# Gate weights folded into the second product of a fused attention and two-MoE kernel

## The chip, the cores and the metric

One core of a Trainium2 chip runs the whole program. The metric is the device time of one execution in microseconds. The kernel before took 864.77, 860.23 and 864.11 us in three runs, median 864.11.

## The reference

Three layers follow each other on 3072 tokens of 384 numbers, in float32:

```python
f = 1 / (1 + exp(-f_logit))                     # (4, 8, 768, 48)
state = f[t][..., None] * state + outer(k[t], v[t])
y[t] = q[t] @ state                             # -> x, (3072, 384)

h = x @ w_in                                    # (384, 2048)
g = h * sigmoid(h)
x2 = g @ w_out                                  # (2048, 384)

logits = x2 @ w_gate                            # (384, 8)
e = argmax(logits);  p = softmax(logits)[e]
out = p * (relu(x2 @ w1[e]) @ w2[e])            # (8, 384, 1024), (8, 1024, 384)
```

The logits are a linear function of g: logits = g @ (w_out @ w_gate). An argmax decides which expert a token gets, so they are computed to about float32's precision.

## The kernel before

**Tiles and groups.** The 24 chunks of 128 tokens are worked on in nine groups, of 2, 2, then six times 3, then 2 chunks (0 to 8). The 2048 columns of w_in, and the rows of w_out, are cut into 16 pieces of 128. Every weight of the MoE layers, and every operand that meets one, is split into a rounded part hi and a rest lo, and each product is three matmuls: hi with lo, lo with hi, hi with hi.

**Slots.** The main loop runs over 144 slots (g, i), a group and a piece: the first 8 pieces of group 0, all 16 of group 1, the other 8 of group 0, then groups 2 to 8. A slot s does `moe_h` (nine matmuls ph for the piece of w_in; 256 or 384 token columns), then the steps that the table `plan` has for s, then `moe_g` (SiLU on ACT and VectorE, and its split gh, gl), then `moe_o` of slot s − 2 (for each tile of the group three matmuls px of 384 columns with the pieces of w_out), then the steps of the table `after`. `plan` is filled by `at(s, ...)` and `after` by `at_end(s, ...)`: attention stages of a later group, loads and splits of weight pieces (`load_piece`; f is the attention's gate input, in_raw and out_raw the raw weight pieces), and the logits. TensorE's instructions keep this written order. The other engines' order is set by the tile framework's scheduler; each engine's queue runs in order, SyncE's loads too.

**Logits.** When a group's last piece is done, `moe_x2` (called at the end of `moe_o`) copies each px times 0.5 into x2 (the SiLU's factor 2 is undone there). For groups 0 to 7 the tiles are then turned one a slot by `flip_rows` (three transposes plt, one ACT copy rt) and at the slot's end multiplied with the gate weights wgc by `gate` (three float32 matmuls of 8 columns, which the chip runs as six passes, and a VectorE copy into lgt). `pick` (argmax, softmax) comes after the last tile's slot, `route` four slots later (rank within the expert, then scatter of the rows by GpSimd into the token buffer xs). Group 8's two tiles get their logits in the tail by `logits_pe` and `logits_pe2`.

**Token buffer.** xs in DRAM has 4096 rows of 388 numbers. Eight transfers of 512 rows (`prefill`) fill it with an empty row, zrow, issued on SyncE's queue from slots 21, 23, ... 35 on of the plan.

**Tail.** A string, TAIL, orders what follows slot 143. Its letters: T start and turn the rows of the first expert's first part ("head", pxs_h), o one `moe_o`, f one up-product (nine matmuls p_h) or down-product (24 matmuls po_h) of the head, l and m the logits of group 8, p `pick`, r `route`, w the load of a second expert's first matrix, k the rank, g the fetch of the rest's rows (xe_r), t their turn (pxs_r), F what is left of f. In `route`, pr is the counting product on TensorE. Then `moe2` runs all the other experts (p_r is the rest's first product).

**Weight tiles.** `new_unit` takes hi and lo of four pieces from one ring of 16 tiles, "wt". zrow, the turned rows rt and the head's buffers hh share the tile "big" at different times.

Of the kernel before, what the change touches and what calls it, by code (L numbers as in the profile page):

```python
# [9 lines left out]
F32 = mybir.dt.float32  # L10
# [14 lines left out]
EARLY = 6  # L25
TB = 'xah'
HB = 'xah'
LB = 'x'
RT = 3
RD = 4  # L30
FA = 1
# [9 lines left out]
KACT = 7  # L41
ND = 1
MO = 'oeh'
TAIL = 'TooflfmfpfrffwgfkfftF'
KW = -14
HF0 = 137
FX = 0
# [19 lines left out]
WE = -6  # L67
WS = -1
PF = 20
PFD = 2  # L70
GACT = 9
PR = 1, 0, 1, 0, 1, 0, 1, 0
PRD = 2
# [18 lines left out]
def kernel(  # L92
# [50 lines left out]
    ends = dram.tile([NCH, DM], F32, name="ends")  # L143
    xs = dram.tile([E * CAP, ROW], F32, name="xs")

    ident = const.tile([P, P], F32, name="ident")
# [14 lines left out]
    big = late.tile([P, 6 * 512], F32R, tag="big", name="big")  # L161
    xt0 = [big[:, i * 2 * DM : (i + 1) * 2 * DM].rearrange("p (r c t) -> p r c t", r=2, c=KC) for i in range(2)]
    zrow = big[:, 4 * DM : 4 * DM + ROW].bitcast(F32)
    BANKS = {0: "haahhaaa", 1: "haahhaaa"}

    def use(n, i, name):
# [31 lines left out]

    def new_unit(key):
        kind = key[0]  # L200
        full = [P, 4, KC, P] if kind in ("in", "w1") else [P, 4, DM]
        nm = "_".join(str(x) for x in key)
        units[key] = tuple(wts.tile(full, F32R, tag="wt", name=f"{nm}_{x}") for x in ("hi", "lo"))

    def part_of(src, kind, i, n):
        cols = slice(i * P, (i + n) * P)
# [2 lines left out]
    def load_raw(t, src, kind, i, eng):  # L209
# [12 lines left out]
    def split(key, h, x, lo_engine):  # L222
        hi, lo = units[key]
        (keep(nc.scalar.copy) if key == ("w1", 1, 1) and RT > 1 else nc.scalar.copy)(hi[:, h], x)  # L224
        lo_engine.tensor_sub(lo[:, h], x, hi[:, h].bitcast(F32))  # L225
# [280 lines left out]
    def moe_o(g, i):  # L506
        hi, lo = gt.pop((g, i))
        first, last = ((0, HF), (HF - 1, NF - 1)) if g == 0 else ((0,), (NF - 1,))
        wh, wl = units["out", i // 4]
        if i in first:  # L510
            px[g] = [bank("x", f"px_{g}_{t}") for t in range(sizes[g])]
        for t in range(sizes[g]):
            o = px[g][t][:, :DM]
            m = slice(t * P, (t + 1) * P)
            pe.matmul(o, hi[:, m], wl[:, i % 4, :], start=i in first, stop=False)
            pe.matmul(o, lo[:, m], wh[:, i % 4, :], start=False, stop=False)
            pe.matmul(o, hi[:, m], wh[:, i % 4, :], start=False, stop=i in last)
# [6 lines left out]
    def moe_x2(g, i):  # L524
        lgt[g] = att.tile([P, sizes[g], E], F32, tag="lg", name=f"lg_{g}", bufs=2)
        for t in range(sizes[g]):
            n = starts[g] + t
            if n in x2:
                nc.vector.scalar_tensor_tensor(
                    out=x2[n][:, :DM], in0=px[g][t][:, :DM], scalar=0.5, in1=x2[n][:, :DM], op0=ALU.mult, op1=ALU.add  # L530
                )
                r = x2[n]
            else:
                r = att.tile([P, ROW], F32, tag="x2", name=f"x2_{n}", bufs=5)
                x2[n] = r
# [8 lines left out]
    rts = []  # L544

    def logits_pe(g):
        for t in range(sizes[g]):
            r = x2[starts[g] + t]
            pt = bank("a", f"plt_{g}_{t}")
            for c in range(KC):  # L550
                pe.transpose(pt[:, c * P : (c + 1) * P], r[:, c * P : (c + 1) * P], ident)
            rt = att.tile([P, KC, P], F32, tag="sg", name=f"rt_{g}_{t}", bufs=SG)
            (keep(nc.scalar.copy) if t % 2 < RT - 1 else nc.vector.tensor_copy)(rt.rearrange("p c t -> p (c t)"), pt[:, :DM])
            rts.append(rt)

    def logits_pe2(g):
        for t, rt in enumerate(rts):
            pl = bank(LB, f"plg_{g}_{t}")
            for c in range(KC):
                pe.matmul(pl[:, :E], rt[:, c, :], wgc[:, c, :], start=c == 0, stop=c == KC - 1)  # L560
            nc.vector.tensor_copy(lgt[g][:, t, :], pl[:, :E])
# [4 lines left out]
    def flip_rows(g, t):  # L566
# [2 lines left out]
        for c in range(KC):  # L569
            pe.transpose(pt[:, c * P : (c + 1) * P], r[:, c * P : (c + 1) * P], ident)  # L570
        if not turned_rows:
            turned_rows.append(late.tile([P, 4, KC, P], F32, tag="big", name="rt"))
        rt = turned_rows[0][:, (starts[g] + t) % 4]
        nc.scalar.copy(rt.rearrange("p c t -> p (c t)"), pt[:, :DM])
        flipped[g, t] = pt, rt

# [221 lines left out]
    def head_start():  # L798
        w = HEAD * P
        xt_hl = [att.tile([P, CPG, KC, P], F32R, tag=f"xt{x}", name=f"xe{x}_h", bufs=2) for x in "hl"]  # L800
        flat = [x.rearrange("p r c t -> p (r c t)") for x in xt_hl]
        big = late.tile([P, 8 * DM], F32R, tag="big", name="hh_h")
        more = [att.tile([P, DM], F32R, tag=x, name=f"{x}_h") for x in ("ep", "en")]
        slots = [big[:, i * w : (i + 1) * w] for i in range(8 * DM // w)]
# [7 lines left out]
    def rest_fetch():  # L812
# [5 lines left out]
        x = wts.tile([P, 2, KC, w], F32R, tag="wt", name="x_r")  # L818
        items["rest"] = dict(nm="r", e=0, w=w, rows=lambda t: r[t], x=[x[:, i] for i in range(2)])

    def moe2(m2):
# [310 lines left out]
    assert s0 + RD < len(seq)  # L1132
    at(HF0, head_fetch)
# [32 lines left out]
    nc.scalar.preload_act_table_set("natural_log_exp_and_others")  # L1166
    consts()
    total = NG * NF
    for s in range(first, total):
        if s >= 0:  # L1170
            moe_h(*seq[s])
# [30 lines left out]
    for c in TAIL:
# [48 lines left out]
```

## Time and profile before

| | before |
|---|---|
| median of three runs | 864.11 us (860.23 to 864.77) |
| profiled execution, its own time | 862.22 us |
| span of the profiled execution | 860.5 us |
| mean granted clock of TensorE | 0.976 |
| TensorE busy | 824.1 us, 96%, 5684 matmuls |
| VectorE busy | 490.9 us, 57% |
| ACT busy | 383.8 us, 45% |
| GpSimd busy | 107.7 us, 13% |
| DMA | 95.93 MB, mean 111 GB/s |

The span is the profiled part of one execution; what lies around it is 1.7 us. Busy time of a matmul counts from its start to its modelled end, and neighbours overlap, so the price of one in a full stream is the step between two starts. [...] PE in a row is TensorE, DVE VectorE, ACT ScalarE, POOL GpSimd, SP or SPq SyncE's queue. L328 is the one line that issues all of TensorE's products, L333 the one for transposes, so rows are told apart by their tiles.

### The profile page before, as it was taken

The page shows a single profiled execution, that of the slowest core. Times are in us where ns is not written, and L with a number is a line of the kernel's source. Part 1 is how long each engine was busy: PE and PEld are TensorE (multiplying, and loading weights), DVE is VectorE, ACT ScalarE, POOL GpSimd, SP SyncE. Part 2 cuts the span into 40 slices and gives each one's busy share as a digit, 9 for nine tenths or more (in the row PEclk, how much of TensorE's full clock was granted, in tenths as well). Part 3 has the DMA queues.
Part 4 walks back from the last instruction along what each step waited for, and adds up shares of the span by engine and source line. Part 5 has one row for each costly group of instructions (what it writes and reads, how often), then busy time and mean ns, then how long its engine had stood idle before and what let it go on. Part 6 is the DMA issues. An engine that isn't in the chain of part 4 may idle for free.

```text
span 860.5 us, 15378 instructions
## 1 busy us (share of the span) xinstructions
PE 824.1 (96%) x5684; PEld 786.9 (91%) x5684; DVE 490.9 (57%) x1290; ACT 383.8 (45%) x803; POOL 107.7 (13%) x136
## 2 busy tenths in 40 slices
PE   6789899999999999999999999999999999999994
PEld 3689899989999999999999999998998999999994
DVE  5898786546566665666567547354456336336520
ACT  5554654353353444435345333355355335335520
POOL 2001000001102001001001101045301110110011
PEclk9779989999999999999999999999999999999998
DMA  9755990222343343344333312214182425525400
GB/s 202 166 147 140 295 240 16 45 42 72 88 103 102 77 99 103 75 93 110 75 82 98 94 52 75 91 38 157 47 274 86 160 77 186 164 81 191 164 26 27
DMA packets 166436, 95.93 MB, mean 111 GB/s; under 512 B 115692, under 2 KB 159965, under 8 KB 166352
## 3 DMA queue, kind: packets, MB, share of 16 engines
q1 hardware_dynamic: 162224, 83.80, 37.3%
q0 software_dynamic: 3280, 9.49, 3.0%
q10 hardware_dynamic: 848, 1.57, 0.6%
q8 instruction: 46, 0.75, 0.4%
q14 instruction: 38, 0.31, 0.1%
HBM read 75.61 MB, written 16.33 MB: 107 GB/s over the span
## 4 chain that ended last, share of the span: by engine, by line
PE 70%; DMA 10%; DVE 6%; issue 5%; ACT 4%; SPq 2%; POOL 1%; POOLq 0%; DVEq 0%; ACTq 0%
PE px L328 20%; PE ph L328 19%; PE po L328 8%; PE p L328 7%; PE py L328 4%; DMA out_dram<-o,oi 3%; DMA f<-in_f_logit_dram 2%; PE sc L328 2%; DMA in_raw<-in_moe_w_in_dram 2%; DMA w_raw<-in_moe_w_dram 2%; PE plt L328 1%; PE pl L328 1%; PE p_r L328 1%; PE po_r L328 1%; PE pxs L333 1%
## 5 line engine op out<-in xcount | busy, mean ns | idle before, releaser
L492 ACT ACTIVATE se<-ph 128x384 f32<-128x384 f32 (+1 forms) x144 | 65.3, 454 | 166.7 <-PE ph L328 162.6
L328 PE MATMUL px<-out_lo,gh 128*128 128x384 f32 x384 | 137.4, 358 | 1.5 <-ACT gh L502 1.2
L494 DVE SCALAR_TENSOR_TENSOR sg<-se,ph 128x384 f32<-128x384 f32 (+1 forms) x144 | 73.0, 507 | 105.6 <-ACT se L492 104.9
L328 PE MATMUL px<-out_hi,gl 128*128 128x384 f32 x384 | 130.8, 341 | 0.6 <-DVE gl L503 0.5
L328 PE MATMUL px<-out_hi,gh 128*128 128x384 f32 x384 | 130.4, 340 | 0.0
L328 PE MATMUL ph<-xtl,in_hi 128*128 128x384 f32 (+1 forms) x384 | 126.0, 328 | 0.0
L328 PE MATMUL ph<-xth,in_lo 128*128 128x384 f32 (+1 forms) x384 | 124.5, 324 | 0.8 <-DVE in_lo L225 0.8
L328 PE MATMUL ph<-xth,in_hi 128*128 128x384 f32 (+1 forms) x384 | 124.7, 325 | 0.0
L503 DVE TENSOR_TENSOR gl<-sg,gh 128x384 fp32r<-128x384 f32 (+1 forms) x144 | 79.9, 555 | 34.1 <-ACT gh L502 33.1
L502 ACT CAST gh<-sg 128x384 fp32r<-128x384 f32 (+1 forms) x144 | 68.6, 477 | 67.4 <-DVE sg L494 64.0
L328 PEld LDWEIGHTS px<-out_lo,gh 128*128 128x128 f32 x384 | 73.0, 190 | 4.4 <-ACT gh L502 1.9
L328 PEld LDWEIGHTS px<-out_hi,gl 128*128 128x128 f32 x384 | 73.3, 191 | 1.1 <-DVE gl L503 1.1
L328 PEld LDWEIGHTS ph<-xth,in_lo 128*128 128x128 f32 x384 | 72.9, 190 | 1.2 <-DVE in_lo L225 1.1
L328 PEld LDWEIGHTS px<-out_hi,gh 128*128 128x128 f32 x384 | 72.9, 190 | 0.0
L328 PEld LDWEIGHTS ph<-xtl,in_hi 128*128 128x128 f32 x384 | 72.8, 190 | 0.0
L328 PEld LDWEIGHTS ph<-xth,in_hi 128*128 128x128 f32 x384 | 72.8, 190 | 0.0
L328 PE MATMUL po<-w_lo,hh 128*128 128x384 f32 (+6 forms) x200 | 67.8, 339 | 0.0
L328 PE MATMUL po<-w_hi,hh 128*128 128x384 f32 (+6 forms) x200 | 67.3, 336 | 0.0
L328 PE MATMUL po<-w_hi,hl 128*128 128x384 f32 (+6 forms) x200 | 67.3, 336 | 0.0
L224 ACT CAST w_hi<-w_raw 128x384 fp32r<-128x384 f32 x124 | 57.1, 513 | 21.7 <-DMA w_raw<-in_moe_w_dram 19.0
L225 DVE TENSOR_TENSOR w_lo<-w_raw,w_hi 128x384 fp32r<-128x384 f32 x104 | 52.7, 552 | 10.8 <-ACT w_hi L224 10.5
L328 PE MATMUL p<-xsl,w_hi 128*128 128x480 f32 (+6 forms) x168 | 58.5, 348 | 0.0
(239 smaller groups left out, 1537.7 us busy)
## 6 DMA issues: line engine op xcount, KB each, us to landing
w_raw<-in_moe_w_dram SPq DMA_DIRECT2D x64, 384.0 KB
xs<-big SPq DMA_DIRECT2D x8, 776.0 KB
out_again<-in_moe_w_out_dram SPq DMA_DIRECT2D x16, 384.0 KB
xe<-xs SPq DMA_DIRECT2D x7, 776.0 KB
out_raw<-in_moe_w_out_dram SPq DMA_DIRECT2D x13, 384.0 KB
f<-in_f_logit_dram SPq DMA_DIRECT2D x24, 192.0 KB
k<-in_k_dram SPq DMA_DIRECT2D x24, 192.0 KB
q<-in_q_dram SPq DMA_DIRECT2D x24, 192.0 KB
```

The costliest lines, as they stand in the source:

```text
L224: (keep(nc.scalar.copy) if key == ("w1", 1, 1) and RT > 1 else nc.scalar.copy)(hi[:, h], x)
L225: lo_engine.tensor_sub(lo[:, h], x, hi[:, h].bitcast(F32))
L328: ins = nc.tensor.matmul(*a, **k)
L333: ins = nc.tensor.transpose(*a, **k)
L492: nc.scalar.activation(e, ph[:, :GT], AF.Tanh, scale=0.5)
L494: nc.vector.scalar_tensor_tensor(out=t, in0=e, scalar=1.0, in1=ph[:, :GT], op0=ALU.add, op1=ALU.mult)
L502: (nc.scalar.copy if g < GACT else nc.vector.tensor_copy)(hi, t)
L503: (nc.gpsimd if (g, i) < LOV else nc.vector).tensor_sub(lo, t, hi.bitcast(F32))
```

## The change

- Each tile of w_out (`new_unit`, kind "out") gets eight more columns, filled with w_out @ w_gate. For each of the 16 pieces `fold_turn` multiplies hi and lo as stationary operand with an identity (six matmuls of 128 columns, so the piece is turned and its halves are added), ACT copies the result into one of two tiles wturn, and `fold_gate` multiplies it with wgc (three float32 matmuls of 8 columns, six passes), after which ACT writes the hi and VectorE the lo of the eight columns. Turns are planned for slots 3 to 10 and 19 to 26, gates for the same slots' ends.
- From group 2 on `moe_o` moves 392 columns, and `moe_x2` takes the logits out of the last eight with one VectorE instruction a tile. `flip_rows` and `gate` stay for groups 0 and 1; `logits_pe` and `logits_pe2` are gone. `pick` and `route` of groups 2 to 7 come three slots earlier.
- `prefill` begins with a GpSimd subtraction that writes a spare column of zrow and reads the last pieces of w_in or w_out; the fills' slots are one apart instead of two.
- The ring of 16 weight tiles becomes two of 8 ("wa" for w_in and w1, "wb" for w_out and w2), "big" is cut into "big" and "side", the identity is made in wturn and copied, and wgc is loaded before slot 0.
- The head's start and turn move from the tail into slot 143, and TAIL is reordered: the letters l and m go, both down-products of the head come after the turn of the rest.

```diff
-TAIL = 'TooflfmfpfrffwgfkfftF'
+TAIL = 'ofofpffrffwgffktfF'
-PFD = 2
+PFD = 1
+PW = (0, 0, 1, 1, 2, 2, 3, 3)
-    wts = main.enter_context(tc.tile_pool(name="wts", bufs=16))
+    wts = main.enter_context(tc.tile_pool(name="wts", bufs=8))
...
+    zrow = side[:, :ROW]
+    spare = side[:, DM + 2 : DM + 3]
+    wturn = [side[:, ROW + i * DM : ROW + (i + 1) * DM] for i in range(2)]
...
-        full = [P, 4, KC, P] if kind in ("in", "w1") else [P, 4, DM]
+        full = [P, 4, KC, P] if kind in ("in", "w1") else [P, 4, DM + E if kind == "out" else DM]
+        tag = "wa" if kind in ("in", "w1") else "wb"
...
+    def fold_turn(i):
+        u, h = divmod(i, 4)
+        pt = bank("a", f"pe_{i}")
+        for c in range(KC):
+            for j, part in enumerate(units["out", u]):
+                pe.matmul(
+                    pt[:, c * P : (c + 1) * P], part[:, h, c * P : (c + 1) * P], identr, start=j == 0, stop=j == 1
+                )
+        nc.scalar.copy(wturn[i % 2], pt[:, :DM])
+        folding[i] = pt
+
+    def fold_gate(i):
+        u, h = divmod(i, 4)
+        hi, lo = (a[:, h, DM : DM + E] for a in units["out", u])
+        o = folding.pop(i)[:, DM : DM + E]
+        for c in range(KC):
+            pe.matmul(o, wturn[i % 2][:, c * P : (c + 1) * P], wgc[:, c, :], start=c == 0, stop=c == KC - 1)
+        nc.scalar.copy(hi, o)
+        nc.vector.tensor_sub(lo, o, hi.bitcast(F32))
...
-            o = px[g][t][:, :DM]
+            w = DM if g < 2 else DM + E
+            o = px[g][t][:, :w]
-            pe.matmul(o, hi[:, m], wl[:, i % 4, :], start=i in first, stop=False)
+            pe.matmul(o, hi[:, m], wl[:, i % 4, :w], start=i in first, stop=False)
...
+            if g >= 2:
+                nc.vector.tensor_scalar(
+                    out=lgt[g][:, t, :], in0=px[g][t][:, DM : DM + E], scalar1=0.5, scalar2=None, op0=ALU.mult
+                )
...
-        for t in range(sizes[g]):
-            at(s0 + t, flip_rows, g, t)
-            at_end(s0 + t, gate, g, t)
-        s0 += sizes[g]
+        if g < 2:
+            for t in range(sizes[g]):
+                at(s0 + t, flip_rows, g, t)
+                at_end(s0 + t, gate, g, t)
+            s0 += sizes[g]
...
+    for i in range(NF):
+        at(i + (3 if i < HF else 11), fold_turn, i)
+        at_end(i + (3 if i < HF else 11), fold_gate, i)
...
-    at(6, lambda: nc.sync.dma_start(out=wgc, in_=moe2_w_gate.rearrange("(c p) e -> p c e", p=P)))
+    at(-4, lambda: nc.sync.dma_start(out=wgc, in_=moe2_w_gate.rearrange("(c p) e -> p c e", p=P)))
...
     def prefill(i):
+        lo = units["in", 3][1][:, :, 0, :1] if i % 2 == 0 else units["out", 3][1][:, :, :1]
+        tc.keep_in_program_order(
+            nc.gpsimd.tensor_sub(spare, lo[:, PW[i]].bitcast(F32), lo[:, PW[i]].bitcast(F32))
+        )
...
+    at(total - 1, head_turn)
```

The order of instructions at three places, before and changed.

TensorE at the end of slot 4, in group 0 or 1, before: the last ph, the six px of slot 2, the first ph of slot 5.

```order
L328 MATMUL ph_4_762<-big,in_hi 128x256
L328 MATMUL px_0_703<-out_lo,gh_2_699 128x384 [waits Activation_49]
L328 MATMUL px_0_703<-out_hi,gl_2_700 128x384 [waits DVE_49]
L328 MATMUL px_0_703<-out_hi,gh_2_699 128x384
L328 MATMUL px_1_704<-out_lo,gh_2_699 128x384
L328 MATMUL px_1_704<-out_hi,gl_2_700 128x384
L328 MATMUL px_1_704<-out_hi,gh_2_699 128x384
L328 MATMUL ph_5_786<-big,in_hi 128x256 [waits DVE_49]
```

Changed: the last two of the fold's six turn matmuls (pe), the same px, the gate passes of the fold, the first ph of slot 5.

```order
L355 MATMUL pe_792<-identr,out_hi 128x128
L355 MATMUL pe_792<-identr,out_lo 128x128
L355 MATMUL px_0_706<-out_lo,gh_2_702 128x384
L355 MATMUL px_0_706<-out_hi,gl_2_703 128x384 [waits DVE_49]
L355 MATMUL px_0_706<-out_hi,gh_2_702 128x384
L355 MATMUL px_1_707<-out_lo,gh_2_702 128x384
L355 MATMUL px_1_707<-out_hi,gl_2_703 128x384
L355 MATMUL px_1_707<-out_hi,gh_2_702 128x384
L355 MATMUL pe_792<-wgc,side 128x8 [waits Activation_49]
L355 MATMUL pe_792<-wgc,side 128x8 x2
L355 MATMUL ph_5_815<-big,in_hi 128x256 [waits DVE_49]
```

Between ph and px stand six matmuls more, and behind px the gate passes, with a wait for ACT; ph of slot 5 is behind them.

TensorE in the tail, before: the end of the first down-product po_h, the turn of the rest's rows pxs_r, the start of the second po_h.

```order
L328 MATMUL po_h_7486<-w_0_1_lo,hh_h 128x384 [waits Activation_49,Pool_49]
L328 MATMUL po_h_7486<-w_0_1_hi,en_h 128x384 [waits DVE_49]
L328 MATMUL po_h_7486<-w_0_1_hi,hh_h 128x384
L333 MATMUL pxs_r_7518<-ident,xe_r_7440 128x128 [waits DMAHW4_49]
L333 MATMUL pxs_r_7518<-ident,xe_r_7441 128x128 [waits DMAHW5_49]
L333 MATMUL pxs_r_7523<-ident,xe_r_7440 128x128 [waits PE_49]
L333 MATMUL pxs_r_7523<-ident,xe_r_7441 128x128
L333 MATMUL pxs_r_7528<-ident,xe_r_7440 128x128
L333 MATMUL pxs_r_7528<-ident,xe_r_7441 128x128
L328 MATMUL po_h_7533<-w_0_0_lo,hh_h 128x384
```

Changed: the end of the last up-product p_h, pxs_r, the first po_h.

```order
L355 MATMUL p_h_7513<-xel_h,w_0_1_hi 128x256
L355 MATMUL p_h_7513<-xeh_h,w_0_1_lo 128x256
L355 MATMUL p_h_7513<-xeh_h,w_0_1_hi 128x256
L360 MATMUL pxs_r_7542<-identr,xe_r_7496 128x128 [waits DMAHW4_49]
L360 MATMUL pxs_r_7542<-identr,xe_r_7497 128x128 [waits DMAHW5_49]
L360 MATMUL pxs_r_7547<-identr,xe_r_7496 128x128 [waits DVE_49,PE_49]
L360 MATMUL pxs_r_7547<-identr,xe_r_7497 128x128
L360 MATMUL pxs_r_7552<-identr,xe_r_7496 128x128 [waits DVE_49]
L360 MATMUL pxs_r_7552<-identr,xe_r_7497 128x128
L355 MATMUL po_h_7557<-w_0_0_lo,hh_big 128x384 [waits Activation_49]
L355 MATMUL po_h_7557<-w_0_0_hi,hh_side 128x384
```

A down-product that stood ahead of the turn, which waits for the fetch's transfers, now stands behind it.

SyncE's queue at the fills, before: f, q and k of attention, five of the fills (xs<-big), and weight pieces of w_in between and behind them.

```order
L191 DMA q_1089<-in_q_dram 128x8x48 [waits DMAHW4_49,DVE_49]
L191 DMA f_1665<-in_f_logit_dram 128x8x48 [waits DMAHW5_49]
L1143 DMA xs<-big 128x4x388 [waits DMAHW6_49]
L1143 DMA xs<-big 128x4x388 [waits DMAHW7_49]
L1143 DMA xs<-big 128x4x388 [waits DMAHW0_49]
L219 DMA in_raw<-in_moe_w_in_dram 96x3x256 [waits DMAHW1_49,DVE_49]
L220 DMA in_raw<-in_moe_w_in_dram 32x3x256 [waits DMAHW2_49]
L1143 DMA xs<-big 128x4x388 [waits DMAHW3_49]
L1143 DMA xs<-big 128x4x388 [waits DMAHW4_49]
L219 DMA in_raw<-in_moe_w_in_dram 96x3x256 [waits DMAHW5_49,DVE_49]
L220 DMA in_raw<-in_moe_w_in_dram 32x3x256 [waits DMAHW6_49]
L351 DMA a_all<-ends 48x4x1 [waits DMAHW7_49]
```

Changed: the last loads around slots 20 to 30, seven of the fills (xs<-side), and one v load among them.

```order
L195 DMA q_1859<-in_q_dram 128x8x48 [waits DMAHW4_49,DVE_49]
L378 DMA a_all<-ends 48x4x1 [waits DMAHW5_49,DMAHW2_49]
L378 DMA a_all<-ends 48x4x1 [waits DMAHW6_49]
L222 DMA out_raw<-in_moe_w_out_dram 128x768 [waits DMAHW7_49,DVE_49]
L1169 DMA xs<-side 128x4x388 [waits DMAHW0_49,Pool_49]
L1169 DMA xs<-side 128x4x388 [waits DMAHW1_49,Pool_49]
L1169 DMA xs<-side 128x4x388 [waits Pool_49]
L1169 DMA xs<-side 128x4x388 [waits DMAHW3_49,Pool_49]
L195 DMA v_1907<-in_v_dram 128x8x48 [waits DMAHW4_49,PE_49]
L1169 DMA xs<-side 128x4x388 [waits DMAHW5_49,Pool_49]
L1169 DMA xs<-side 128x4x388 [waits DMAHW6_49,Pool_49]
L1169 DMA xs<-side 128x4x388 [waits DMAHW7_49,Pool_49]
```

Each fill waits for GpSimd, whose queue has these rows: the empty row is made, then one subtraction for each fill, from the second on behind the DMA of the fill before.

```order
L1161 MEMSET side 128x388 [waits Pool_49]
L1162 MEMSET side 128x1 [waits Pool_49]
L1167 TENSOR_TENSOR side<-in_lo 128x1 [waits DVE_49]
L1167 TENSOR_TENSOR side<-out_lo 128x1 [waits DMAHW7_49,DVE_49,Pool_49]
L1167 TENSOR_TENSOR side<-in_lo 128x1 [waits DMAHW0_49,Pool_49]
L1167 TENSOR_TENSOR side<-out_lo 128x1 [waits DMAHW1_49,DVE_49,Pool_49]
```

The fills have moved behind the last weight piece (out_raw) but for the first, and v and k loads stand behind or between them.

## Rows read from the trace of the kernel before

**Rows 1.** The page's slices, 40 of 21.5 us: TensorE's busy tenths, granted clock, DMA share

```profile
PE   6789899999999999999999999999999999999994
...
PEclk9779989999999999999999999999999999999998
DMA  9755990222343343344333312214182425525400
```

**Rows 2.** Stretches: length; busy PE, PEld, DVE, ACT, POOL; granted clock; DMA share, GB/s

```profile
80.00:100.00 20.00, 20.00 (x166) 19.76 (x167) 18.47 (x50) 11.42 (x28) 1.73 (x4) 1.00 0.90 239
100.00:120.00 20.00, 17.50 (x111) 16.98 (x108) 13.06 (x30) 11.44 (x21) 0.00 (x0) 0.83 1.08 310
```

**Rows 3.** Groups of instructions, ACT: busy us, mean ns, idle before and releaser

```profile
L574 ACT COPY rt<-plt 128x384 f32<-128x384 f32 x22 | 10.5, 476 | 3.5 <-PE plt L333 3.5
```

**Rows 4.** TensorE's timeline in a slot of group 3: start us, us, instruction

```profile
240.10 0.34 PE L328 MATMUL px<-out_lo,gh 128*128 128x384 f32 x1
...
240.62 0.73 PE L328 MATMUL plt<-wgc,rt 128*128 128x8 f32 x6
241.20 0.42 PE L328 MATMUL ph<-xtl,in_hi 128*128 128x384 f32 x1
241.46 0.34 PE L328 MATMUL ph<-xth,in_lo 128*128 128x384 f32 x1
...
242.85 0.49 PE L333 MATMUL plt<-ident,x 128*128 128x128 f32 x3
243.10 0.42 PE L328 MATMUL px<-out_lo,gh 128*128 128x384 f32 x1
243.35 0.33 PE L328 MATMUL px<-out_hi,gl 128*128 128x384 f32 x1
```

**Rows 5.** The same view in a slot of group 8, whose chunks are two

```profile
555.87 0.28 PE L328 MATMUL ph<-xtl,in_hi 128*128 128x256 f32 x1
...
556.22 0.28 PE L328 MATMUL ph<-xtl,in_hi 128*128 128x256 f32 x1
```

**Rows 6.** TensorE's waits: total us, times, longest

```profile
PE plt L328 <- ACT rt L574: 2.9, 2, 1.9
...
PE px L328 <- ACT gh L502: 1.2, 2, 1.0
PE ph L328 <- DVE in_lo L225: 0.8, 1, 0.8
PE pk L333 <- ACT qt L375: 0.7, 1, 0.7
PE px L328 <- DVE gl L503: 0.5, 1, 0.5
PE pxs_r L333 <- DMA xe_r<-xs: 0.5, 1, 0.5
```

**Rows 7.** TensorE's timeline, products of qt with the state

```profile
326.17 1.03 PE L328 MATMUL py<-qt,state 112*112 112x128 f32 x8
327.13 0.31 PE L328 MATMUL py<-am,v 128*48 128x128 f32 x1
```

**Rows 8.** SyncE's timeline at three of the fills: start us, us

```profile
98.30 2.53 SPq L1143 DMA_DIRECT2D xs<-big  x3
```

**Rows 9.** The chain there, a weight piece: start us, us, what

```profile
102.28 6.97 DMA in_raw<-in_moe_w_in_dram
```

**Rows 10.** Stretches of the hole, columns as in group 2

```profile
100.00:104.00 4.00, 1.50 (x16) 1.09 (x12) 3.58 (x7) 2.58 (x3) 0.00 (x0) 1.00 1.04 368
104.00:112.00 8.00, 8.00 (x39) 8.00 (x40) 2.56 (x6) 3.43 (x7) 0.00 (x0) 0.57 1.04 324
```

**Rows 11.** The chain of the tail, columns as in group 9

```profile
608.99 0.11 PE pr L328 x4
...
618.56 0.77 PE pxs_r L333 x5
```

**Rows 12.** A stretch of the tail, columns as in group 2

```profile
600.00:604.00 4.00, 3.86 (x18) 3.86 (x19) 1.93 (x7) 1.69 (x5) 4.00 (x5) 0.57 0.30 96
```

More of the change, by code (lines that the diff above doesn't have):

```diff
@@ L27 @@
 HB = 'xah'
-LB = 'x'
 RT = 3
@@ L144 @@
     xs = dram.tile([E * CAP, ROW], F32, name="xs")
-    ident = const.tile([P, P], F32, name="ident")
+    identr = const.tile([P, P], F32R, name="identr")
+    ident = identr.bitcast(F32)
     trir = const.tile([P, P], F32R, name="trir")
@@ L160 @@
     wgc = const.tile([P, KC, E], F32, name="wgc")
-    big = late.tile([P, 6 * 512], F32R, tag="big", name="big")
+    big = late.tile([P, 4 * DM], F32R, tag="big", name="big")
+    side = late.tile([P, 10 * P], F32, tag="side", name="side")
     xt0 = [big[:, i * 2 * DM : (i + 1) * 2 * DM].rearrange("p (r c t) -> p r c t", r=2, c=KC) for i in range(2)]
-    zrow = big[:, 4 * DM : 4 * DM + ROW].bitcast(F32)
+    zrow = side[:, :ROW]
+    spare = side[:, DM + 2 : DM + 3]
+    wturn = [side[:, ROW + i * DM : ROW + (i + 1) * DM] for i in range(2)]
     BANKS = {0: "haahhaaa", 1: "haahhaaa"}
@@ L200, in new_unit @@
         kind = key[0]
-        full = [P, 4, KC, P] if kind in ("in", "w1") else [P, 4, DM]
+        full = [P, 4, KC, P] if kind in ("in", "w1") else [P, 4, DM + E if kind == "out" else DM]
         nm = "_".join(str(x) for x in key)
-        units[key] = tuple(wts.tile(full, F32R, tag="wt", name=f"{nm}_{x}") for x in ("hi", "lo"))
+        tag = "wa" if kind in ("in", "w1") else "wb"
+        units[key] = tuple(wts.tile(full, F32R, tag=tag, name=f"{nm}_{x}") for x in ("hi", "lo"))
     def part_of(src, kind, i, n):
@@ L220, in load_raw @@
         eng.dma_start(out=t[96:], in_=x[KC * 96 :].rearrange("(c p) f -> p c f", c=KC))
[L222 to L225, printed above, removed]
     def load_piece(kind, i):
@@ L247, in load_piece, with split @@
         split((kind, u), h, x if kind == "in" else x[:, 0], nc.vector)
+    def split(key, h, x, lo_engine):
+        hi, lo = (a[:, h] if key[0] != "out" else a[:, h, :DM] for a in units[key])
+        (keep(nc.scalar.copy) if key == ("w1", 1, 1) and RT > 1 else nc.scalar.copy)(hi, x)
+        lo_engine.tensor_sub(lo, x, hi.bitcast(F32))
+    folding = {}
+    def fold_turn(i):
[16 more added lines that the diff above has]
+        nc.vector.tensor_sub(lo, o, hi.bitcast(F32))
     def verify_piece(kind, i, s):
@@ L512, in moe_o @@
         for t in range(sizes[g]):
-            o = px[g][t][:, :DM]
+            w = DM if g < 2 else DM + E
+            o = px[g][t][:, :w]
             m = slice(t * P, (t + 1) * P)
-            pe.matmul(o, hi[:, m], wl[:, i % 4, :], start=i in first, stop=False)
-            pe.matmul(o, lo[:, m], wh[:, i % 4, :], start=False, stop=False)
-            pe.matmul(o, hi[:, m], wh[:, i % 4, :], start=False, stop=i in last)
+            pe.matmul(o, hi[:, m], wl[:, i % 4, :w], start=i in first, stop=False)
+            pe.matmul(o, lo[:, m], wh[:, i % 4, :w], start=False, stop=False)
+            pe.matmul(o, hi[:, m], wh[:, i % 4, :w], start=False, stop=i in last)
         if i in last:
@@ L542, in moe_x2 @@
         del px[g]
-    rts = []
-    def logits_pe(g):
-        for t in range(sizes[g]):
[L548 to L561, printed above, removed]
     flipped = {}
@@ L571, in flip_rows @@
         if not turned_rows:
-            turned_rows.append(late.tile([P, 4, KC, P], F32, tag="big", name="rt"))
-        rt = turned_rows[0][:, (starts[g] + t) % 4]
+            turned_rows.append(late.tile([P, 3, KC, P], F32, tag="side", name="rt"))
+        rt = turned_rows[0][:, (starts[g] + t) % 3]
         nc.scalar.copy(rt.rearrange("p c t -> p (c t)"), pt[:, :DM])
@@ L801, in head_start @@
         flat = [x.rearrange("p r c t -> p (r c t)") for x in xt_hl]
-        big = late.tile([P, 8 * DM], F32R, tag="big", name="hh_h")
-        more = [att.tile([P, DM], F32R, tag=x, name=f"{x}_h") for x in ("ep", "en")]
-        slots = [big[:, i * w : (i + 1) * w] for i in range(8 * DM // w)]
+        bigs = [late.tile([P, n * w], F32R, tag=x, name=f"hh_{x}") for x, n in (("big", 6), ("side", 5))]
+        more = [att.tile([P, DM], F32R, tag=x, name=f"{x}_h") for x in ("ep", "en", "in_q")]
+        slots = [x[:, i * w : (i + 1) * w] for x, n in zip(bigs, (6, 5)) for i in range(n)]
         slots += [x[:, KC * w : (KC + 1) * w] for x in flat] + [x[:, :w] for x in more]
@@ L817, in rest_fetch @@
             keep(nc.sync.dma_start)(out=r[t], in_=slots_of(0, HEAD + t, 1).rearrange("n p d -> p (n d)"))
-        x = wts.tile([P, 2, KC, w], F32R, tag="wt", name="x_r")
+        x = wts.tile([P, 2, KC, w], F32R, tag="wb", name="x_r")
         items["rest"] = dict(nm="r", e=0, w=w, rows=lambda t: r[t], x=[x[:, i] for i in range(2)])
@@ L1062, in consts @@
     def consts():
-        make_identity(nc, ident)
+        make_identity(nc, wturn[0][:, :P])
+        nc.vector.tensor_copy(identr, wturn[0][:, :P])
         t = att.tile([P, P], F32, tag="lft", name="tri0")
@@ L1122 @@
         s0 = {0: L0, 1: L1}.get(g, pos[g, NF - 1] + LAG + 1)
-        for t in range(sizes[g]):
-            at(s0 + t, flip_rows, g, t)
-            at_end(s0 + t, gate, g, t)
-        s0 += sizes[g]
+        if g < 2:
[3 more added lines that the diff above has]
+            s0 += sizes[g]
         at(s0, pick, g)
@@ L1132, with head_turn @@
     assert s0 + RD < len(seq)
+    for i in range(NF):
+        at(i + (3 if i < HF else 11), fold_turn, i)
+        at_end(i + (3 if i < HF else 11), fold_gate, i)
+    def head_turn():
+        head_start()
+        turn(items["head"])
     at(HF0, head_fetch)
@@ L1187, in fill @@
         del ops[:n]
-    def start():
-        head_start()
-        turn(items["head"])
     def preload():
@@ L1197 @@
     todo = dict(
-        T=start, o=lambda: moe_o(*outs.pop(0)), f=lambda: fill(1), F=lambda: fill(len(ops)), l=lambda: logits_pe(g),
-        m=lambda: logits_pe2(g), p=lambda: pick(g), r=lambda: route(g), w=preload, k=rank_rest,
+        o=lambda: moe_o(*outs.pop(0)), f=lambda: fill(1), F=lambda: fill(len(ops)),
+        p=lambda: pick(g), r=lambda: route(g), w=preload, k=rank_rest,
         g=rest_fetch, t=lambda: turn(items["rest"]),
```

## Prediction

> **What bounds the kernel now.** I read the page first. Its slices of 21.5 us [rows 1] show TensorE at 9 tenths or more from the fourth on, but for an 8 in the fifth and the last slice, and the granted clock near full but for a 7 in the second and third and an 8 in the sixth. So almost every matmul that is removed or added counts at its own price, and what is not TensorE's counts only where TensorE stands still. I then read the stretches [rows 2]: from 80 to 100 us TensorE has 20.00 of 20 us (VectorE 18.47, nearly full too), and from 100 to 120 only 17.50, at a granted clock of 0.83, with the DMA share over 1. The fills are issued ahead of that hole. Then I read the prices of single instructions from TensorE's timeline, the waits, and the chain at the end.
>
> **Prices.** The busy time of a matmul contains pipelining, so I take the step from start to start. Three products px of 384 columns take 240.62 − 240.10 = 0.52 us, 0.173 each [rows 4]. Three ph of 256 columns take 556.22 − 555.87 = 0.35, 0.117 each [rows 5]. The difference over 128 columns is 0.44 ns a column.
>
> **Logits taken out.** Per tile: three transposes step 0.25 (242.85 to 243.10) and the next px 0.25 instead of 0.173, so 0.33; six gate passes step 0.58 (240.62 to 241.20) and the next ph 0.26 instead of 0.173, so 0.67 [rows 4]. Together 1.00 us. Groups 2 to 7 have 18 tiles that lose both: −18.0. TensorE waited twice for the copy rt, 2.9 us in all [rows 6]; the longer, 1.9 us, is at a tile of the first two groups, which keep their transposes, so −1.0 more. Sum −19.0. The ACT copies of 476 ns [rows 3] and the VectorE copies lie beside and are worth nothing: TensorE is the fuller engine in those stretches.
>
> **Columns added.** 20 tiles × 16 pieces × 3 products = 960 matmuls, 8 columns each: 960 × 8 × 0.44 ns = +3.4. The new VectorE instruction of 8 columns per tile is hidden under the next slot's products.
>
> **The fold.** Sixteen pieces each get six turn matmuls (stationary 128×128, 128 moving columns), one ACT copy and six gate passes. The gate passes have the form of the old ones: 0.67. A turn matmul in this form is not in the trace. From below it is bounded by the transpose, 0.25/3 = 0.082 [rows 4]; nearest from above is the product of qt with state, also 128 moving columns, eight in 0.96 us, 0.12 each [rows 7]. Further off, it can hardly cost more than a px of three times the columns, 0.173. I take 0.10, midway between the two near rows: 6 × 0.10 + 0.08 = 0.68. Piece: 1.35; sixteen: +21.6 (19.8 at 0.082, 23.5 at 0.12, 31 at 0.173). It is not hidden: slots 3 to 10 lie in the third and fourth slice, at 8 and 9 tenths [rows 1], in a stretch that flows into the full one [rows 2], and slots 19 to 26 come behind the hole, at 9.
>
> [...]
>
> **The gate's wait.** Gate passes of the fold wait for the ACT copy. They are behind the slot's six px, 6 × 0.173 = 1.04 us, against 0.48 for the copy [rows 3] and a hop on either side, so most are covered. The old gates had the same form of cover and lost 2.9 us in 22 tiles, 0.13 each: 16 × 0.13 = +2.1. Ends: 0, and 0.5 a piece (8) if ACT, which has the slot's activations and weight casts in one line, gets to the copy late. What stands behind a waiting gate is all of TensorE.
>
> **The fills.** All eight leave their place between the loads in SyncE's queue ahead of and in the hole (three in the row shown), where a weight piece issued behind them takes 6.97 us to land [rows 8, 9]. TensorE loses 4.00 − 1.50 = 2.5 us of idle time from 100 to 104, and then runs 8 us at 0.57 of full clock, (1 − 0.57) × 8 = 3.4 [rows 10]. Both should go: −5.9. Two other small waits of the same kind of cause (in_lo 0.8, qt 0.7 [rows 6]) are swallowed by a TensorE that is later by the folds: −1.5. Sum −7.4; the other end is 0, if the late loads are late for other reasons. The eight fills become a chain, each waiting on POOL for the one before, after the last weight pieces; they are then in slices with a DMA share of 0 to 2 tenths [rows 1], but SyncE's in-order queue holds the v and k loads of the next chunks behind them. I cost this at nothing, since those slices leave the loads room to be late; without that cover it is a few us. The ring of 16 weight tiles cut into two of 8, the identity made by way of another tile and the earlier gate load I also cost at nothing: the same tiles are held as long, and the users come later.
>
> **The tail.** Group 8 loses its two tiles' transposes and gates: −2.0. Its route comes nearer to px, but the work that covered the road from the counting product pr to the rest's rows is cut: before, pr at 608.99 and the first transposes of the rest at 618.56, 9.6 us apart [rows 11], had four up-products (36 matmuls) and one whole po_h between them and lost 0.5 [rows 6]. Now 36 × 0.117 = 4.2 us stand there, since both po_h come after the transposes. The road is DVE, POOL's two scatters, their landing, the fetch and its landing; nothing of it is shortened. So 9.6 − 4.2 = 5.4 of wait, less the 0.5 that is paid already: +4.9. After a stop the clock is low: after 2.5 us of idle it cost 3.4 us [rows 10]; I take 3.4 again. In return the px waits before the last slots (gh 1.2, gl 0.5 [rows 6]) should go, since the weight loads that crowd ACT there are issued earlier, and with them the low clock of 600 to 604, (1 − 0.57) × 4 = 1.7 [rows 12]: −3.4. Tail: −2.0 + 4.9 + 3.4 − 3.4 = +2.9.
>
> **Sum.** 862.2 (the profiled execution) − 19.0 + 3.4 + 21.6 + 2.1 − 7.4 + 2.9 = 865.8. That execution is 1.9 below the median of the runs, 864.1, and inside their spread. About 0.5%, 4.3 us, is what a measurement of this kernel can tell from no change: 859.8 to 868.4. I forecast **866 us**: the fold costs TensorE a little more than the logits gave, and the fills' stop pays for the columns and the tail.
>
> **Rivals.**
> - *Slower: the gates stand.* In slots 3 to 10 ACT and VectorE are busy with weight pieces. If the copy ends over 1.04 us after the turn, each gate stops all of TensorE, at 0.5 us or more: 8 instead of 2.1, and the stops bring the clock down as in [rows 10], say one such fall, 3.4: 866 + 5.9 + 3.4 = 875. The turn at 0.173 instead would give 875 as well. For it: VectorE's 18.47 of 20 [rows 2], and the two waits on rt [rows 6]. Against: only two waits in 22. Chance 0.24. [...]
> - *Faster: cheap turns, a short tail.* The turn at 0.082 (−1.8), gates never waiting (−2.1), the road from pr shorter by 2 us because DVE and POOL are freer, and the clock not falling after it (−5.4): 866 − 9.3 = 857. For it: the transposes' price and a POOL that has less to split late. Against: the road's DMA parts don't shrink, and every stop in the trace brought a low clock. Chance 0.20.
> - *The fills' move does nothing.* The loads that TensorE waited for around 100 us are late because the whole early stretch moves that many bytes (share 0.90 already before 100 us [rows 2]); −7.4 shrinks to nothing: 873. Against: fills are much of what moved there. Chance 0.08.
> - The forecast has 0.48.
>
> **Numbers.** Range 856 to 875, from just past the faster rival to the slower ones. Faster than 859.8: 0.18 of the faster rival and 0.03 of the forecast, 0.21. Slower than 868.4: 0.22 and 0.07 of the rivals and 0.05 of the forecast, 0.34. The rest, 0.45.
>
> **What would show it.** Timeline of TensorE in slot 4 or 5: turns stepping 0.08 to 0.12 and no idle before the gate's first pass; 0.2 or a wait named ACT would be the slower rival. From 100 to 120 us a TensorE at 20 of 20 and full clock; a hole there would kill the fills' term. Slots of three tiles in groups 2 to 7 at 18 × 0.173 + 9 × 0.0035 = 3.15 us. In the tail one wait of some 5 us before the rest's transposes, released by the fetch's DMA, and a clock near 0.5 behind it; no such wait means the tail term is wrong by up to 8. Products px of 392 columns stepping 0.177; 0.19 or more would make the columns cost (0.19 − 0.177) × 960 = 12 us more than I gave them.

## The result and the profile after

The changed kernel takes 874.38 us, median of four runs (871.21 to 878.09), against 862.17 for the kernel before (859.60 to 864.77). The ratio is 1.0149, with an interval of 1.0117 to 1.0182: slower by about 12 us. The forecast was 866, no change; the time lies at the upper end of the range, and it is the time of the rival to which I gave the smallest chance, 0.08: the fills' move does nothing, 873. The slower rival, gates that stand, had 875, but its sign is absent: no gate waits, as shown below.

The profiled execution is the longest of the four, 878.09 us with a span of 876.4. The page's slices, as in [rows 1], now of 21.9 us each:

```profile
PE   6889989999999999999999999999799999999994
...
PEclk9667979999999999999999999999899999999997
DMA  9763336412235325326324332314173425425400
```

The busy digits hardly differ. The granted clock has lost tenths in the second to fourth slice (6, 6, 7) and has a 7 in the sixth. DMA's two nines at the fifth and sixth slice have gone: the fills are spread over later slices, as planned. What the eye looks for is the hole of [rows 2], and it has not gone, only moved:

```profile
100.00:120.00 20.00, 18.25 (x143) 17.83 (x142) 13.36 (x36) 13.55 (x28) 0.00 (x0) 0.99 0.44 90
120.00:140.00 20.00, 19.24 (x115) 19.01 (x116) 17.64 (x45) 9.28 (x25) 0.55 (x2) 0.75 0.66 188
```

TensorE is busy 18.25 and 19.24 of 20 us, the second with a granted clock of 0.75, and the DMA share is 0.44 in the first, where it was 1.08. So the transfers left and the hole stayed.

The first ph of a slot gives the clearest account. These are starts in TensorE's timeline (us from the span's start) of the kernel before, of the changed kernel's first profile and of a second one (experiment "The change once more" below):

| start of slot | before | changed | later by | changed, 2nd | later by |
|---|---|---|---|---|---|
| 3 | 52.16 | 52.71 | 0.6 | 51.91 | −0.3 |
| 11 (behind eight folds) | 86.45 | 103.72 | 17.3 | 96.14 | 9.7 |
| 16 | 98.20 | 115.55 | 17.4 | 107.97 | 9.8 |
| 17 (behind the hole) | 109.07 | 127.71 | 18.6 | 120.13 | 11.1 |
| 27 (behind all folds) | 138.98 | 166.05 | 27.1 | 158.65 | 19.7 |
| 139 | 584.63 | 595.57 | 10.9 | 588.39 | 3.8 |
| 143 | 593.07 | 605.59 | 12.5 | 598.30 | 5.2 |
| end of the span | 860.5 | 876.4 | 15.9 | 868.0 | 7.5 |

**The fold.** Slots 8, 9 and 10 are each 1.33 to 1.34 us longer than before, and 24, 25 and 26 are 1.32 to 1.36; the forecast was 1.35 for a piece. TensorE's timeline in slot 10, changed kernel (start, duration):

```profile
97.53 0.33 PE L355 MATMUL pe<-identr,out_hi 128*128 128x128 f32 x1
97.69 0.28 PE L355 MATMUL pe<-identr,out_lo 128*128 128x128 f32 x1
...
98.03 0.28 PE L355 MATMUL pe<-identr,out_hi 128*128 128x128 f32 x1
...
98.25 0.39 PE L355 MATMUL px<-out_lo,gh 128*128 128x384 f32 x1
...
99.17 0.33 PE L355 MATMUL px<-out_hi,gh 128*128 128x384 f32 x1
99.34 0.73 PE L355 MATMUL pe<-wgc,side 128*128 128x8 f32 x6
99.92 0.36 PE L355 MATMUL ph<-xtl,in_hi 128*128 128x256 f32 x1
```

The first turn to the fifth, 97.53 to 98.03, and the step of the later ones, (98.25 − 97.69)/5 = 0.112, stand between the two rows that bounded the price, 0.082 and 0.12. The gate's six passes step 0.58 as before, and no idle time is noted ahead of them: the wait that I gave 2.1 us does not exist here.

**The hole.** TensorE's timeline in slot 16, and below it VectorE's, both of the changed kernel:

```profile
116.70 1.16 PE L355 MATMUL sc<-qt,kt 48*128 48x128 f32 x16
117.79 0.46 PE L355 MATMUL py<-state,qt 112*128 112x96 f32 x2
120.76 1.25 PE L355 MATMUL py<-v,am 128*128 128x48 f32 x4 [2.50 <-DVE am L422]
```

```profile
117.99 0.42 DVE L521 SCALAR_TENSOR_TENSOR sg<-se,ph 128x256 f32<-128x256 f32 x1 [0.84 <-ACT se L519]
118.33 0.55 DVE L323 SCALAR_TENSOR_TENSOR out_cv<-out_raw,out_cv 128x384 uint32<-128x384 uint32 x1
118.88 0.42 DVE L530 TENSOR_TENSOR gl<-sg,gh 128x256 fp32r<-128x256 f32 x1
119.22 0.55 DVE L326 SCALAR_TENSOR_TENSOR out_cv<-out_raw,out_cv 128x384 uint32<-128x384 uint32 x1
119.69 0.41 DVE L521 SCALAR_TENSOR_TENSOR sg<-se,ph 128x256 f32<-128x256 f32 x1
120.02 1.28 DVE L422 TENSOR_TENSOR am<-sc,trir 128x512 f32<-128x512 f32 x2
```

The scores sc end near 117.9, TensorE does two products with the state and then stands 2.50 us until am, the masked scores. VectorE gets to am at 120.02, because two steps of a w_out piece's split (out_cv), and sg, gl and the next sg of the SiLU, are ahead of it in its queue. No transfer is among them. The five fill VectorE without a gap from 117.99 us on, and am starts behind the last of them.

The same place in the kernel before, TensorE's timeline and then VectorE's:

```profile
102.42 0.42 PE L328 MATMUL py<-v,am 128*128 128x48 f32 x2 [1.52 <-DVE am L395]
103.83 0.42 PE L328 MATMUL py<-v,am 128*128 128x48 f32 x2 [0.98 <-DVE am L395]
```

```profile
101.01 0.76 DVE L315 TENSOR_SCALAR f<-f 128x1152 f32<-128x1152 f32 x1 [0.19 <-DMA f<-in_f_logit_dram]
101.69 0.68 DVE L395 TENSOR_TENSOR am<-sc,trir 128x512 f32<-128x512 f32 x1
...
102.62 0.55 DVE L299 SCALAR_TENSOR_TENSOR out_cv<-out_raw,out_cv 128x384 uint32<-128x384 uint32 x1
103.09 0.68 DVE L395 TENSOR_TENSOR am<-sc,trir 128x512 f32<-128x512 f32 x1
```

The two waits, 1.52 and 0.98, are all of the 2.5 us that I had put down to late loads. VectorE itself stood only 0.19 us there for a transfer. Over the whole span am is what TensorE waited for longest (total us, times, longest):

```profile
PE py L328 <- DVE am L395: 6.7, 8, 1.9
```

In the changed kernel the clock falls behind the wait; in stretches, columns as in [rows 2]:

```profile
116.00:120.00 4.00, 2.25 (x25) 1.83 (x23) 3.15 (x8) 2.81 (x6) 0.00 (x0) 0.95 0.01 4
120.00:130.00 10.00, 9.24 (x39) 9.15 (x40) 7.64 (x19) 2.06 (x7) 0.24 (x1) 0.51 0.42 110
```

A px steps 0.32 us there (126.11 to 126.43, clock 0.50) against 0.175 ahead of the wait (114.50 to 114.85 in two steps, clock 1.00). What a low clock loses, here as in the forecast, is my estimate: the stretch times one less its granted clock; by these two steps it is 0.45 of the stretch at a clock of 0.50.

**The tail.** pr, the turn of the rest's rows and TensorE's wait for it:

```profile
616.22 0.18 PE L355 MATMUL pr<-r_ohb,stri 128*128 128x16 bf16 x1
...
625.68 1.84 PE L360 MATMUL pxs_r<-identr,xe_r 128*128 128x128 f32 x6 [4.86 <-DMA xe_r<-xs]
```

```profile
620.00:626.00 6.00, 1.14 (x9) 0.80 (x7) 2.04 (x11) 0.57 (x2) 1.29 (x2) 0.90 0.41 132
626.00:632.00 6.00, 5.96 (x22) 5.81 (x22) 1.27 (x3) 1.12 (x3) 0.00 (x0) 0.53 0.00 0
```

The stretches are those of the wait and of the 6 us behind it. The wait is 4.86 us, the forecast was 5.4, and the clock behind it is 0.53 for 6 us, (1 − 0.53) × 6 = 2.8 us lost where I took 3.4.

### The profile page after: what moved, and what is told of

Same layout as the page of the kernel before. It is cut to its first block, busy times and chain, and to the rows that moved or that the text cites. A ratio compares the mean times of both kernels' runs of the same rounds, so it can differ in the third digit from the quotient of the medians.

```text
span 876.4 us, 15480 instructions
## 1 busy us (share of the span) xinstructions
PE 839.1 (96%) x5696; PEld 801.3 (91%) x5696; DVE 492.3 (56%) x1307; ACT 383.6 (44%) x815; POOL 109.9 (13%) x144
## 5 line engine op out<-in xcount | busy, mean ns | idle before, releaser
L355 PE MATMUL px<-out_lo,gh 128*128 128x392 f32 (+1 forms) x384 | 137.8, 359 | 0.0
L355 PE MATMUL px<-out_hi,gl 128*128 128x392 f32 (+1 forms) x384 | 132.1, 344 | 1.6 <-DVE gl L530 1.6
L355 PE MATMUL px<-out_hi,gh 128*128 128x392 f32 (+1 forms) x384 | 131.7, 343 | 0.0
```

The source lines that it names most:

```text
L355: ins = nc.tensor.matmul(*a, **k)
```

## The experiments

A time of the kernel before stands beside each: 861.18 us (25 runs) for the fills alone, the scores alone, the down-product first and the folds in another place, 861.20 (24 runs) for the others.

**Do the fills make the hole?** Kernel before, the fills held back until the last weight pieces are split:

```diff
     def prefill(i):
+        if i == 0:
+            spare = big[:, 5 * DM + 2 : 5 * DM + 3]
+            for kind in ("in", "out"):
+                lo = units[kind, 3][1][:, 3] if kind == "out" else units[kind, 3][1][:, 3, 0]
+                lo = lo[:, :1].bitcast(F32)
+                tc.keep_in_program_order(nc.gpsimd.tensor_sub(spare, lo, lo))
```

> The kernel before with only the fills moved: GpSimd makes the empty row wait for the last pieces of w_in and w_out, and all eight fills follow at once. Nothing else is changed. The prediction's step (the loads that the fills hold up make the hole of 100 to 112 us) expects the hole gone, TensorE at 20 of 20 us and full clock from 98 to 118, and 862 - 6 = 856 us. The rival expects the hole to stay: in the trace of before the two waits of 1.5 and 1.0 us there are put down to VectorE's masked scores (am), and in the changed kernel, where no fill is near, slot 16 still waits 2.5 us for am and takes 12.2 us against 10.9 before. It expects a wait for am of 1.5 to 2.5 us in slot 16, a clock near 0.5 for some 7 us behind it, and 860 to 864 us.

Measured: 863.28 us (10 runs), ratio 1.0029 (1.0001 to 1.0057): no gain, rather 2 us more. The hole is there, and the wait is longer. TensorE's and VectorE's timelines:

```profile
98.69 0.46 PE L328 MATMUL py<-state,qt 112*128 112x96 f32 x2
103.23 0.66 PE L328 MATMUL py<-v,am 128*128 128x48 f32 x2 [4.08 <-DVE am L395]
```

```profile
100.96 0.35 DVE L293 TENSOR_SCALAR in_cv<-in_raw 128x384 uint32<-128x384 uint32 x1
...
101.56 0.55 DVE L296 SCALAR_TENSOR_TENSOR out_cv<-out_raw,out_cv 128x384 uint32<-128x384 uint32 x1
102.03 0.55 DVE L296 SCALAR_TENSOR_TENSOR in_cv<-in_raw,in_cv 128x384 uint32<-128x384 uint32 x1
102.50 0.68 DVE L395 TENSOR_TENSOR am<-sc,trir 128x512 f32<-128x512 f32 x1
```

Without the fills ahead of them, the last pieces of w_in are issued from 90.7 us on instead of from 100.9, and VectorE now has steps of two pieces (in_cv and out_cv) ahead of am: 4.08 us of waiting in place of 1.5 and 1.0. Slot 16 takes 14.1 us instead of 10.9. Slots 17 to 26 together take 27.5 instead of 29.9, so behind the hole the move does give something, and the hole takes it. The prediction's step falls, the rival stands.

**Is it the order of scores and product?** Kernel before, one number:

```diff
-ST5 = (7, 10, 12, 16, 16, 18)
+ST5 = (7, 10, 12, 15, 16, 18)
```

> The kernel before with one number changed: the score products of the sixth chunk move from slot 16 to slot 15; the product that needs the masked scores stays in slot 16. In slot 16 both stood in one slot, with nothing between them on TensorE but two products with the state. If the hole is that dependency, the masking now lies beside the px of slot 15 and the ph of slot 16, 2.1 us of TensorE's work; the wait for am goes, the clock stays up, and the time is 862 - 6 = 856 us. If the fills cause the hole, it stays (or moves to the next load that is late) and the time is 862.

Measured: 863.15 us (10 runs), ratio 1.0024 (0.9994 to 1.0055), no gain. But the hole is gone: slot 17 starts 6.0 us earlier than before, of which this execution had 1.2 at slot 15 already, so the edit gives 4.8. A stretch, and the waits:

```profile
96.00:104.00 8.00, 8.00 (x71) 7.88 (x71) 5.72 (x13) 5.10 (x8) 0.00 (x0) 1.00 1.01 297
```

```profile
PE ph L328 <- ACT in_hi L224: 3.6, 3, 1.9
...
PE ph L328 <- DVE in_lo L225: 1.6, 3, 0.7
```

TensorE is at 8.00 of 8 us there, with a DMA share of 1.01 beside it; further on it now waits 3.6 us for in_hi and 1.6 for in_lo, in slots 20, 21 and 23, and at slot 24 it is only 0.6 us ahead. The cause of the hole is shown: scores, mask and product in one slot, and the mask behind other work in VectorE's queue. What stood behind it is the supply of weight pieces.

**Both together.** Kernel before, both edits:

> The kernel before with both the fills moved behind the last weight pieces and the scores a slot earlier. Each alone left the time at 863. With the scores early, TensorE waited 5.2 us for weight pieces of w_in in slots 19 to 22. If those pieces are late because the fills take the transfers and SyncE's queue ahead of them, moving the fills pays now: no waits named in_hi or in_lo, slots 16 to 23 without a hole, and 861 - 5 to 7 = 854 to 856 us. If the pieces are late for VectorE's and ACT's sake (the splits), the waits stay and the time is 860 to 863.

Measured: 856.07 us (11 runs, 854.98 to 860.70), ratio 0.9935 (0.9917 to 0.9954). This is less than both kernels take. In slots 17 to 22, columns as above:

```profile
104.00:112.00 8.00, 7.64 (x58) 7.47 (x57) 7.89 (x20) 5.14 (x14) 0.00 (x0) 1.00 0.70 183
112.00:120.00 8.00, 8.00 (x65) 7.75 (x64) 8.00 (x21) 3.56 (x9) 0.99 (x1) 1.00 0.51 139
```

A wait of 1.23 us for am is left in slot 16, the clock stays at 1.00, and no wait names in_hi or in_lo. From slot 15 to slot 27 it takes 36.8 us, the kernel before 42.9. So the fills did hold up the weight pieces, but their move pays only once the hole ahead of them is gone: together the edits give 5 us, alone neither gives anything.

**The order of the tail**, both ways. Changed kernel, the head's first down-product ahead of the rest's turn:

```diff
-TAIL = 'ofofpffrffwgffktfF'
+TAIL = 'ofofpffrffwgffkftF'
```

> The changed kernel with one letter of the tail's string moved: the head's first down-product (24 matmuls, 4.2 us) stands ahead of the rest's turn again, as before the change. The changed kernel's profile waits 4.9 us for the rest's rows there, and the clock is low behind it. If the tail's order is what costs there, the wait shrinks to about 0.7, the clock stays up, and the time is 874 - 4 to 7 = 867 to 870 us. If the rest's rows are late for another reason, for which the down-product waits too, the wait moves and the time stays at 874.

Measured: 866.01 us (10 runs), ratio to before 1.0048 (1.0023 to 1.0073), so 6 to 8 us less than the changed kernel in its two series (874.4 above, 872.4 below). The wait is 0.78 us and the clock 1.00 behind it:

```profile
618.00:624.00 6.00, 5.11 (x31) 4.63 (x30) 1.10 (x4) 1.51 (x4) 0.97 (x1) 1.00 0.38 121
```

From slot 143 to the end of the span it takes 263.7 us, the changed kernel 270.8 and 269.7 in its two profiles, the kernel before 267.4. So the rest of the tail's change is worth 3.7 from there on, and the order alone costs 6 to 7.

Kernel before, the opposite edit:

```diff
-TAIL = 'TooflfmfpfrffwgfkfftF'
+TAIL = 'TooflfmfpfrffwgfkftfF'
```

> The kernel before with one letter of the tail's string moved: the first down-product of the head behind the turn of the rest, the order that the change has. If that order is the whole of the tail's loss, TensorE waits 4.2 + 0.5 = 4.7 us for the rest's rows, the clock is near 0.5 for some us behind it, and the time is 861 + 4 to 8 = 865 to 869 us. If the tail's loss comes from the rest of the change (the route, the splits on GpSimd), it is about 861 to 863.

Measured: 868.36 us (6 runs), ratio 1.0064 (1.0035 to 1.0092), so 7 us more than before. The wait and the clock behind it are those of the changed kernel:

```profile
618.60 0.48 PE L333 MATMUL pxs_r<-ident,xe_r 128*128 128x128 f32 x1 [4.64 <-DMA xe_r<-xs]
```

```profile
619.00:625.00 6.00, 5.80 (x22) 5.73 (x22) 1.27 (x3) 1.12 (x3) 0.00 (x0) 0.54 0.00 0
```

**The folds in another place.** Changed kernel:

```diff
     for i in range(NF):
-        at(i + (3 if i < HF else 11), fold_turn, i)
-        at_end(i + (3 if i < HF else 11), fold_gate, i)
+        at(i + 18, fold_turn, i)
+        at_end(i + 18, fold_gate, i)
```

> The changed kernel with the sixteen folds in slots 18 to 33 instead of 3 to 10 and 19 to 26; nothing else. In the changed kernel's profile the folds cost 1.34 us in most slots, but slots 3 to 7 grow by 2.0, 3.8, 3.6, 1.4 and 1.9 at a granted clock of 0.5 from 59 to 75 us. If the folds bring that low clock or lengthen it, slots 0 to 17 fall back to the times of before (slot 17 at 113 instead of 131 us), the folds cost 16 x 1.34 = 21.4 in the new place, and the time is 874 - 6 = 868 us (less in runs where the low stretch was short already). If the low clock comes from something else in the change (the start, the loads), it stays, and the time is 874.

Measured: 873.33 us (4 runs, 872.13 to 874.20), ratio 1.0141 (1.0083 to 1.0198). The time is that of a miss for the theory that the folds bring the low clock and so cost 6 us. Slots 3 to 10 do fall back to the lengths of before, and slot 17 starts at 110.0, but the folds cost as much in their new place, 1.24 to 1.35 each in slots 27 to 33: at slot 34 this kernel is at 175.7 us, and so is the changed kernel in its second profile. The hole stays too, with a longer wait for am; slot 16 takes 14.1 us against 12.2 in the changed kernel, which alone would hide 1.9 of a gain, so the low clock is settled by the next experiment and not by this one:

```profile
102.71 0.66 PE L355 MATMUL py<-v,am 128*128 128x48 f32 x2 [4.10 <-DVE am L422]
```

```profile
98.00:114.00 16.00, 11.62 (x64) 11.18 (x63) 13.84 (x33) 6.72 (x17) 0.24 (x1) 0.68 0.59 169
```

**The change once more**, unedited.

> The changed kernel once more, unedited. Its first profile had a low clock from 59 to 75 us (8 us lost against a full one, where the kernel before lost 2), and was the longest of its four runs, 878.1 against 871.2 to 876.2. The kernel with the down-product first, which has the same instructions up to the tail, shows a clock of 0.94 to 1.00 from 58 us on. If that stretch belongs to single executions and not to the change, this profile has it short or not at all and slots 3 to 10 grow by 1.34 us each and no more; the median lies between 871 and 875. If the folds make it, it is there again, 10 us or longer.

Measured: 872.36 us (869.84 to 873.41), ratio 1.0120 (1.0088 to 1.0152). The same stretch in the first and in the second profile of the changed kernel:

```profile
58.00:76.00 18.00, 18.00 (x87) 17.15 (x87) 11.09 (x27) 7.29 (x19) 0.00 (x0) 0.53 0.46 117
```

```profile
58.00:76.00 18.00, 17.55 (x156) 16.62 (x155) 16.40 (x41) 10.43 (x27) 1.21 (x2) 1.00 0.68 161
```

18 us of the same kernel, at 0.53 in one execution and at 1.00 in the other. So the 7.6 us by which the first profile is later at slot 11 belong to that execution. Whether longer low stretches come more often with the folds than without is open: timed runs show a mean clock only.

**The change with the scores early and the down-product first.**

> The changed kernel with two edits: the scores of the sixth chunk a slot earlier (slot 15 instead of 16), and the head's first down-product ahead of the rest's turn. In the kernel before, the first edit alone emptied the hole (slot 16 came 6.0 us earlier) but the weight pieces of w_in were then late in slots 19 to 22 and took 5.8 us back. In the changed kernel TensorE comes to those slots over 10 us later through the folds, and the fills are behind those pieces. If the theory is right (VectorE's queue makes the hole, the late pieces are the limit behind it), nothing is given back: against the run with the down-product first alone (866.0) the time falls by the wait of 2.5 us and the low clock behind it, to 859 or 860 us. If the limit behind the hole is the same as in the kernel before, it stays at 865 or 866.

Measured: 864.39 us (12 runs, 860.78 to 866.40), ratio 1.0031 (1.0013 to 1.0049). That is 1.6 less than with the down-product alone, not 6, and the two intervals overlap; in the profiles, slots 15 and 16 together take 11.8 us against 14.3. The expectation misses because the hole has only shrunk:

```profile
113.05 0.42 PE L355 MATMUL py<-v,am 128*128 128x48 f32 x2 [1.27 <-DVE am L422]
```

```profile
116.00:122.00 6.00, 6.00 (x25) 6.00 (x25) 3.05 (x9) 1.83 (x5) 0.00 (x0) 0.51 0.79 189
```

TensorE still waits 1.27 us for am, and here the clock does fall, to 0.51 for 6 us, 2.9 us. Against the best kernel, 856.07, this one is 8.3 us longer: 2.9 are this clock, and sixteen folds (21.4 at 1.34 each) cost more than the 16 or so that logits and columns give back.

## Why the prediction was wrong

- **The fills** are the step that failed: "Both should go: −5.9". I read a DMA share of 1.04 to 1.08 beside a TensorE at rest as its cause. The waits view put that time down to VectorE's am, in the row shown above that I did not quote, and I did not look at VectorE's queue. Slot 16 became 1.3 longer instead. The rival with this result had the wrong reason as well: the early bytes were not the cause, and the fills' move did free the pieces ("Both together"), behind a hole that hid it. The smaller part of the term came true in size: the waits for in_lo (0.8) and qt (0.7) have gone or shrunk to 0.2. With the fills alone moved, in_lo's goes and qt's stays at 0.7.
- **The fold**: 21.6 forecast, 16 × 1.34 = 21.4 by the six slots named above. A turn steps 0.112, where I took 0.10. The sum at 0.173 was wrong: 16 × (6 × 0.173 + 0.08 + 0.67) is 28.6 and not 31, so that form of the slower rival gave 873 and not 875. **The gate's wait**: 2.1 forecast, none measured.
- **Logits and columns**: −19.0 + 3.4 = −15.6 forecast. From slot 27 to slot 139 the changed kernel gains 27.1 − 10.9 = 16.2 in one profile and 19.7 − 3.8 = 15.9 in the other. This term was right.
- **The tail**: +2.9 forecast; from slot 139 to the end it is 5.0 and 3.7. The mechanism was right and the order's cost was sized well (8.3 forecast with the clock; 6 to 7 by one experiment, and by the other 7 in the times and 9.4 in the profile). The wait was read a little too long: 618.56 in [rows 11] is the start of the last five transposes, and the first starts at 618.10, so the wait comes to 4.9, as measured. The gains were a little too high: the wait ahead of px did not go but moved (for gl, 1.25 us, in slot 139).
- **The clock**: that every stop in the trace of before brought a low clock is a misreading: behind stops of 0.83 us at 127 us and 0.99 at 568 the granted clock is 1.00. The price of the tail's clock rested on the stop of 2.5 us and held nearly (2.8 for 3.4).
- **Together**: 865.8 with −5.9 taken out, 1.3 for the longer hole, −2.1 for the gates and 0.8 to 2.1 for the tail is 871.7 to 873.0, against medians of 874.4 and 872.4. An early low clock as in the first profile, which no term had, may be the rest of the first median; that it was there in the unprofiled runs is not shown.

## What to carry to other kernels

Where an engine stands beside a busy resource, look at what released it and at what stood ahead of that in the releaser's queue; a full DMA beside it (a share of 1.04 here) does not make it the cause. A product that needs another engine's answer to the product just ahead of it wants a slot's work between them, and even that left 1.2 to 1.3 us of waiting where other work stood ahead of the mask in VectorE's queue. Of two limits behind each other, removing one can give nothing (863 us with either edit here, 856 with both): read what is waited for next and try both. A step hoisted ahead of the cover that hid a transfer costs the cover's length (here 4.2 us of products, 4.9 us of waiting), and here the low clock behind the stop too (0.53 for 6 us).

## What was not expected of the hardware

- The same stretch of 18 us of the same kernel ran at a granted clock of 0.53 in one execution and at 1.00 in another, with TensorE busy 18.00 and 17.55 of 18 us.
- A stop of 1.23 us left the clock at 1.00 ("Both together"), one of 1.27 brought it to 0.51 (the changed kernel with the scores early and the down-product first), and one of 1.54 at 212 us of the changed kernel left it at 1.00. So the length of a stop alone does not tell.
- A fill of 776 KB lands 4.6 us after its issue when the fills go one by one (changed kernel). The eight are issued from 128 to 165 us, the second at 139 behind the last piece of w_out, and no wait of TensorE names them or a load held up behind them.
